# Retention attention and a gated MLP on one core: 64-row chunks on two half-partitions become 128-row chunks on all 128 partitions

## The chip, the cores and the metric

The kernel runs on one core of a Trainium2 chip. The metric is the device time in microseconds (us); the kernel before is given as the median of three runs. Beside the times there is one profiled execution of the kernel, taken by the hardware profiler; its span is a little shorter than the metric.

The engines are named as in the profile: PE (TensorE matmuls), PEld (its weight loads), DVE (VectorE), ACT (ScalarE), POOL (GpSimd) and SP (SyncE, here the engine that issues nearly all DMAs).

## The reference, cut to what matters

```python
# attention: B, H, S, D = 8, 8, 576, 64
scores = q @ k.T / sqrt(D)
gamma  = 1.0 - 2.0 ** (-5.0 - arange(H))
Dmat   = where(rel >= 0, gamma ** rel, 0.0)      # rel = t - s
attn   = (scores * Dmat) @ v                     # no softmax
x      = attn.transpose(0, 2, 1, 3).reshape(B, S, 512)

# gated MLP: w_in [512, 1024], w_sg [576, 576], w_out [512, 512]
h    = gelu(x @ w_in)                            # tanh form
u, v = h[..., :512], h[..., 512:]
v_n  = (v - mean(v)) / sqrt(var(v) + 1e-6) * g_ln
v_s  = einsum('ts,bsd->btd', w_sg, v_n) + b_sg[None, :, None]
out  = x + (u * v_s) @ w_out                     # [8, 576, 512], float32
```

The decay `gamma ** (t - s)` splits into a power of the query's row times a power of the key's row. So attention can go through each sequence chunk by chunk: inside a chunk a masked product of scores and values, and from all earlier chunks one 64x64 state matrix per head.

## The kernel before, in words

All work is cut into jobs, one engine each. An order written out as a long string of job numbers (`ORDER`) says in which sequence the jobs are emitted; `fN` in it puts N units of warming matmuls (`scr`, line 357, on zeros; a unit is 128 columns) on PE. Each engine runs its own instructions in that sequence and waits by semaphores. SP is one such queue: a DMA that waits for its data or for a free buffer holds up the DMAs behind it.

The 8 sequences are done in four pairs. A pair has 1152 rows and is 9 tiles of 128 rows in the MLP (36 tiles in all); the middle tile holds the last 64 rows of the first sequence and the first 64 of the second. In attention a pair is 5 blocks (`RB`): two blocks of 256 rows of the first sequence, the middle block with 64 rows of each, and two blocks of 256 rows of the second. A block's rows lie on 128 partitions as two chunks of 64 rows (in a block of 256 rows a partition holds 2 neighbouring rows), so that all attention matmuls work on 64x64 tiles of PE, four at a time.

What happens to a block, in the names of the profile:

- **Loads** (lines 457 and 460, `ld`, `ldq`): q, k, v of the block from HBM on SP's queue. In a block of 256 rows, two neighbouring rows of 64 floats make one run of 512 B in k and v, and four of q, loaded for two blocks at once (`ldq`), make 1024 B. The middle block's loads have runs of 256 B on 64 partitions each.
- **Prep** (lines 493 and 503): k is cast to bf16 (`kb`), q and v are multiplied by their powers `gpow` (`qb`, `vb`), mostly on POOL.
- **T** (line 540): q and k are transposed by PE into PSUM (`pp`) and copied by DVE (`qT`, `kT`). For the last pair's blocks of 256 rows this is done by four DMA transposes on SP's queue instead (line 560).
- **S** (line 591): scores of the chunk into `pp`; DVE multiplies them by the mask (`ret`, line 604).
- **Z** (line 627): k transposed times v, the chunk's contribution to the state, into `zp`; DVE adds it to the running sum (`run`), and a bf16 copy is made (`zb`).
- **O** (line 673): state times q plus masked scores times v into one `pp`. It comes in two halves, `a_O` and `a_O2`: the second writes the other PSUM bank of each tile, and a semaphore (`swap`) or a drain of PE stands between the two. ACT copies the output, which is x transposed, into `xT` (line 730).

The MLP on a tile:

- `hv` (line 741): x times the v half of `w_in`; gelu on ACT (`vg`), mean and variance on DVE (`bst`, `mv`), four small operations on POOL (`mv`, lines 761 to 764), and the normalised bf16 `vn` (`vmid` for the middle tile) on ACT (line 776).
- `hu` (line 788): the u half of `w_in` times x transposed, gelu on ACT into `uT`.
- `wp` (line 807): `w_sg` along the sequence, times `vn`; per sequence 4 column blocks by 2 halves of 288 rows by 5 tiles, 320 matmuls over all. It needs all tiles of its sequence normalised. DVE multiplies the result into `uT` (line 817). `w_sg` is transposed by PE at the start, once for each sequence of a pair, since their rows lie differently on the tiles (`wtp`, line 921, 50 matmuls).
- `op` (line 838): `uT` times `w_out`. The residual x is added from `xT`: in the first pair by matmuls with the identity (line 833), afterwards from a DMA transpose of `xT` (`xr`, line 847, 27 of them) that DVE adds when it writes `ob` (line 855). `ob` is stored on SP's queue (line 860).

`wp` of the first sequence of a pair can start after the middle block, that of the second after the fifth.

The block's shape, and the load that goes with it, in the code before:

```python
    RB = [(2, 0, ((0, 0), (0, 128))), (2, 2, ((0, 256), (0, 384))),
          (1, MID, ((0, 512), (1, 0))),
          (2, 5, ((1, 64), (1, 192))), (2, 7, ((1, 320), (1, 448)))]
    ...
        if ns == 2:
            e, r0 = ch[0]
            s_ = 4 if sup else 2
            nc.sync.dma_start(f_[:], src[2 * p + e, :, r0:r0 + 128 * s_, :].rearrange("h (p s) d -> p h (s d)", s=s_))
        else:
            for c, (e, r0) in enumerate(ch):
                nc.sync.dma_start(f_[64 * c:64 * c + 64, :, :D], src[2 * p + e, :, r0:r0 + 64, :].rearrange("h p d -> p h d"))
```

Of the kernel before, what the change touches and what calls it, by code (L numbers as in the profile page):

```python
# [19 lines left out]
FETCH = (5400.0, 5000.0)  # L20
# [46 lines left out]
class Job:  # L67
    def __init__(self, eng, dur, due, fn, deps=(), new=None, uses=(), mode=None, nbytes=0, run=0, what="", behind=None, since=0.0, lag=0.0, ins=0, port=False, parts=1):
# [12 lines left out]
class Planner:  # L81
# [50 lines left out]
    def place(self, j, t):  # L132
# [19 lines left out]
        else:  # L152
            late = 0.0
            if j.eng == "PE":
                while self.count + j.ins > 256 * self.block:
# [3 lines left out]
                    self.landed += FETCH[self.landed > 32000.0]  # L159
# [11 lines left out]
    def follow(self, order):  # L171
        line = {e: [] for e in self.free}
        for x in order.split():
            j = self.fill(int(x[1:]), 0.0 if x[0] == "f" and self.warm else 2700.0) if x[0] == "f" else self.jobs[int(x)]
            self.warm = self.warm or x[0] == "f"
            line[j.eng].append(j)
# [58 lines left out]
def kernel(  # L235
# [21 lines left out]
    MID = NT // 2  # L257
    HS = S // 2
    SB = (S + 127) // 128
    NB0 = S - 128 * MID  # L260
# [4 lines left out]
    outf = out.rearrange("b s d -> (b s) d")  # L265

    BUFS = dict(ld=8, ldq=2, qb=2, kb=2, vb=3, qT=2, kT=2, ret=4, zb=6, run=4, xT=2, uT=2, vg=3, mv=3, vn=11, ob=4,
# [6 lines left out]
    def new(tag, shape, dtype):  # L274
# [3 lines left out]
    RB = [(2, 0, ((0, 0), (0, 128))), (2, 2, ((0, 256), (0, 384))),  # L278
          (1, MID, ((0, 512), (1, 0))),
          (2, 5, ((1, 64), (1, 192))), (2, 7, ((1, 320), (1, 448)))]  # L280
    NBK = len(RB)
    XP = 1
    TBQ, TBK = 15, 15
    JOINT = (0, 1)
# [3 lines left out]
    wnat = consts.tile([128, SB, S + 128], BF, name="wnat")  # L288
# [9 lines left out]
    msk4 = consts.tile([128, 2, 4, 32], BF, name="msk4")  # L298
    msk2 = consts.tile([128, 2, 2, 64], BF, name="msk2")
    msk1 = consts.tile([128, 64], BF, name="msk1")  # L300
    NQ, NV = 13, 2 * NBK
    srow_i = consts.tile([128, NQ + NV], I32, name="srow_i")
    srow = consts.tile([128, NQ + NV], F32, name="srow")
    lngt = consts.tile([128, H], F32, name="lngt")
    gpow = consts.tile([128, (NQ + NV) * H], F32, name="gpow")
# [3 lines left out]
    wT = [[consts.tile([128, S], BF, name=f"wT{e}_{j}") for j in range(SB)] for e in range(2)]  # L309
# [7 lines left out]
    nc.gpsimd.iota(srow_i[:, :8], pattern=[[64, 2], [1, 4]], base=-ORG, channel_multiplier=4)  # L317
    nc.gpsimd.iota(srow_i[:, 9:13], pattern=[[256, 2], [1, 2]], base=-ORG, channel_multiplier=2)
    for o, r0 in ((NQ, 0), (NQ + 6, 64)):
        nc.gpsimd.iota(srow_i[:, o:o + 4], pattern=[[-256, 2], [-1, 2]], base=ORG - r0, channel_multiplier=-2)  # L320
    for e in range(2):
        R = slice(64 * e, 64 * e + 64)
        nc.gpsimd.iota(srow_i[R, 8:9], pattern=[[1, 1]], base=RB[2][2][e][1] - ORG, channel_multiplier=1)
        nc.gpsimd.iota(srow_i[R, NQ + 4:NQ + 6], pattern=[[-1, 2]], base=ORG - RB[2][2][e][1], channel_multiplier=-1)
# [5 lines left out]
    def powers(o, n, w):  # L330
        return gpow[:, H * o:H * (o + n * w)].rearrange("p (n h s) -> p n h s", n=n, h=H)

    for o, n, w in ((0, 2, 4), (8, 1, 1), (9, 2 + NBK, 2)):
        g = powers(o, n, w)
        nc.vector.tensor_tensor(g, srow[:, o:o + n * w].rearrange("p (n s) -> p n s", n=n).unsqueeze(2).to_broadcast([128, n, H, w]),
                                lngt[:].unsqueeze(1).unsqueeze(3).to_broadcast([128, n, H, w]), op=Alu.mult)
# [100 lines left out]
    def joint(b):  # L437
        return b % NBK == 2 or b in JOINT

# [766 lines left out]
```

## Time and profile before

| | |
|---|---|
| time, median of 3 runs | 212.62 us (212.53 to 215.94) |
| span of the profiled execution | 211.4 us, 7911 instructions |
| median less span | 1.2 us |
| TensorE's granted clock | full from about 21 us on |
| DMA | 48.4 MB, 85910 packets |

Each line of the profile's groups and of the timeline gives line, engine, operation, output and inputs by name, the tile of PE in rows and columns (64*64, 64*128 or 128*128), and the shape of the output. A group's duration on PE is a latency: matmuls overlap, so the price of one is the distance between the starts of groups. "x16" counts instructions. In rows of windows, the columns are the window, its length, the busy time of PE, PEld, DVE, ACT and POOL with their counts, the granted clock, the mean busy share of the DMA engines (it can exceed 1), and GB/s.

### The profile page before, as it was taken

The numbers are of one execution on the slowest core, as the hardware profiler recorded it, in microseconds if no ns is written. First come the engines' busy times: TensorE is split into PE (matmuls) and PEld (weight loads), VectorE is DVE, ScalarE is ACT, GpSimd is POOL, SyncE is SP. The second block draws the span as 40 slices with busy tenths as digits, with TensorE's granted clock in tenths as the row PEclk, the third lists the DMA queues.
The fourth block names the chain that finished last, engine by engine and source line by source line (L and its number), as shares of the span: only waits on it lengthen the run. The fifth ranks groups of instructions, "written<-read, shape, count | busy, mean of one in ns | idle before, by whom it ended". The sixth has DMA issues, their size and how long they took to land.

```text
span 211.4 us, 7911 instructions
## 1 busy us (share of the span) xinstructions
PE 197.6 (93%) x3384; PEld 137.8 (65%) x3416; DVE 152.5 (72%) x291; ACT 116.8 (55%) x207; POOL 118.3 (56%) x169
## 2 busy tenths in 40 slices
PE   7939999988999999999999999999999999999992
PEld 6727586666676677666767677566677675656661
DVE  3296498877888287967888875897865688576673
ACT  5230598892486954579585452776248349334400
POOL 8735158998667859993769679147582313022000
PEclk9985999999999999999999999999999999999999
DMA  6999999999899999999999999999999902586655
GB/s 164 335 276 305 170 374 295 231 291 340 192 248 296 296 324 276 214 328 189 243 285 109 243 307 206 198 323 182 222 172 148 270 0 78 149 153 174 176 172 198
DMA packets 85910, 48.37 MB, mean 229 GB/s; under 512 B 37035, under 2 KB 79283, under 8 KB 85875
## 3 DMA queue, kind: packets, MB, share of 16 engines
q1 hardware_dynamic: 85856, 47.87, 97.3%
q8 instruction: 26, 0.43, 0.9%
q14 instruction: 10, 0.07, 0.2%
q10 hardware_dynamic: 18, 0.00, 0.0%
HBM read 32.79 MB, written 9.44 MB: 200 GB/s over the span
## 4 chain that ended last, share of the span: by engine, by line
PE 79%; DVE 9%; issue 3%; POOL 3%; DMA 3%; ACT 1%; DVEq 0%; SPq 0%; POOLq 0%
PE wp L807 17%; PE hu L788 13%; PE op L838 13%; PE hv L741 12%; PE scr L357 6%; PE pp L673 6%; PE pp L591 4%; PE pp L540 3%; DMA ld<-in_v_dram 3%; DVE ret L604 2%; PE zp L627 2%; POOL vb L503 1%; DVE bst L756 1%; PE op L833 1%; POOL qb L503 1%
## 5 line engine op out<-in xcount | busy, mean ns | idle before, releaser
L807 PE MATMUL wp<-wT,vn 128*128 128x288 bf16 x256 | 41.1, 286 | 0.7 <-issue 0.6
L503 POOL TENSOR_TENSOR vb<-ld,gpow 128x1024 bf16<-128x1024 f32 (+1 forms) x20 | 34.5, 1731 | 11.6 <-DMA ld<-in_v_dram 8.8
L604 DVE TENSOR_TENSOR ret<-pp,msk 128x1024 bf16<-128x1024 f32 x32 | 38.3, 1215 | 3.4 <-PE pp L591 3.4
L788 PE MATMUL hu<-xT,w_in 128*128 128x256 bf16 (+1 forms) x320 | 36.8, 262 | 0.2
L817 DVE TENSOR_TENSOR uT<-wp,uT 128x288 bf16<-128x288 f32 x64 | 27.6, 451 | 12.4 <-PE wp L807 11.2
L741 PE MATMUL hv<-w_in,xT 128*128 128x512 bf16 x122 | 34.7, 380 | 1.7 <-ACT xT L730 0.3
L838 PE MATMUL op<-w_out,uT 128*128 128x512 bf16 (+1 forms) x138 | 34.4, 373 | 0.6 <-issue 0.2
L776 ACT ACTIVATE vn<-vg,mv 128x512 bf16<-128x512 f32 x32 | 25.3, 809 | 15.3 <-POOL mv L764 15.2
L748 ACT ACTIVATE vg<-hv 128x512 f32<-128x512 f32 x36 | 21.3, 596 | 21.8 <-PE hv L741 16.6
L788 PEld LDWEIGHTS <-w_in 128*128 128x128 bf16 x320 | 28.1, 98 | 7.2 <-issue 0.8
L756 DVE BATCH_NORM_STATS2 bst<-vg 128x6 f32<-128x512 f32 x36 | 24.7, 685 | 9.3 <-ACT vg L748 9.3
L730 ACT ACTIVATE xT<-pp 128x512 bf16<-128x512 f32 (+1 forms) x40 | 20.8, 550 | 18.1 <-PE pp L673 18.1
L807 PEld LDWEIGHTS <-vn 128*128 128x128 bf16 x256 | 24.4, 98 | 9.6 <-issue 0.7
L761 POOL TENSOR_SCALAR mv<-mv 128x2 f32<-128x2 f32 (+1 forms) x20 | 4.5, 224 | 44.7 <-DVE mv L757 37.8
L503 POOL TENSOR_TENSOR qb<-ldq,gpow 128x1024 bf16<-128x1024 f32 x14 | 26.9, 1934 | 4.0 <-DMA ldq<-in_q_dram 4.0
L798 ACT ACTIVATE uT<-hu 128x512 bf16<-128x512 f32 x36 | 21.2, 594 | 13.0 <-PE hu L788 12.9
L855 DVE TENSOR_TENSOR ob<-op,xr 128x512 f32<-128x512 f32 (+1 forms) x28 | 18.4, 669 | 8.3 <-PE op L838 6.3
L838 PEld LDWEIGHTS <-uT 128*128 128x128 bf16 x148 | 13.7, 98 | 11.3
L741 PEld LDWEIGHTS <-xT 128*128 128x128 bf16 x144 | 13.2, 98 | 12.0 <-ACT xT L730 0.2
L807 PE MATMUL wp<-wT,vmid 128*128 128x288 bf16 x64 | 18.0, 287 | 0.1
L357 PE MATMUL scr<-warm 128*128 128x256 f32 (+1 forms) x52 | 16.5, 489 | 1.2 <-DVE warm L316 1.2
L357 PEld LDWEIGHTS scr<-warm 128*128 128x128 f32 x52 | 13.0, 271 | 3.9 <-DVE warm L316 1.2
(100 smaller groups left out, 261.7 us busy)
## 6 DMA issues: line engine op xcount, KB each, us to landing
out_dram<-ob SPq DMA_DIRECT2D x35, 256.0 KB, 3.5
ld<-in_k_dram SPq DMA_DIRECT2D x16, 512.0 KB, 6.9
ld<-in_v_dram SPq DMA_DIRECT2D x16, 512.0 KB, 7.0
ldq<-in_q_dram SPq DMA_DIRECT2D x7, 1024.0 KB, 9.6
xT<-in_moe_w_sg_dram SPq DMA_DIRECT2D x2, 576.0 KB, 8.4
ld<-in_q_dram SPq DMA_DIRECT2D x2, 512.0 KB, 7.0
xT<-in_moe_w_in_dram SPq DMA_DIRECT2D x1, 1024.0 KB, 8.0
ld<-in_k_dram SPq DMA_DIRECT2D x8, 128.0 KB, 6.0
```

Source lines behind the costliest of these rows:

```text
L357: nc.tensor.matmul(scr[:, :w], warm[:, :128], warm[:, :w], start=True, stop=True, skip_group_check=True)
L503: ve.tensor_tensor(dst, src, g.unsqueeze(len(src.shape) - 1).to_broadcast(list(src.shape)), op=Alu.mult)
L604: ins = nc.vector.tensor_tensor(ret[:].rearrange("p r (k t) -> p (r k) t", k=2), sc[:].rearrange("p r (k t) -> p (r k) t", k=2), (msk2 if ...
L741: ins = nc.tensor.matmul(hv[:], xTs[p][:, m, kk, :], w_in[:, kk, F2:], start=(kk == 0), stop=(kk == KK - 1))
L748: unfence(nc.scalar.activation(vgs[i][:], cur.pop(("hv", i))[:], Act.Gelu_apprx_tanh), ("V", i))
L756: nc.vector.bn_stats(bst[:], vgs[i][:])
L776: nc.scalar.activation(vn[:], vg[:], Act.Identity, scale=mv[:, s, 2:3], bias=mv[:, s, 3:4])
L788: ins = nc.tensor.matmul(hu[:, n, :], w_in[:, kk, 128 * c:128 * c + 128], xTs[p][:, m:m + w, kk, :], start=(kk == 0), stop=(kk == KK - 1), ...
L798: unfence(nc.scalar.activation(uTs[p][:, c0:c1, 128 * m:128 * m + 128 * w], cur.pop(("hu", i, half))[:], Act.Gelu_apprx_tanh), ("U", i, half))
L807: ins = nc.tensor.matmul(ps[:], vns[t0 + j][e][:, 128 * c:128 * c + 128], wT[e][j][:, half * HS:(half + 1) * HS], start=(j == 0), stop=(j ...
L817: ins = nc.vector.tensor_tensor(uTs[p][:, c, col:col + HS], cur.pop(("wp", b, c, half))[:], uTs[p][:, c, col:col + HS], op=Alu.mult)
L838: ins = nc.tensor.matmul(op[:], uTs[p][:, c, r], w_out[:, c, cs], start=(p >= XP and c == 0), stop=(c == KK - 1), skip_group_check=True)
```

## The change

**Rows.** A chunk now has 128 consecutive rows, one row on each of 128 partitions. The half block comes first: the first 64 rows of both sequences of the pair, one on each half of the partitions. Four full blocks of two chunks follow (`NS`). In the first pair a full block holds two chunks of one sequence, as before; from the second pair on (`SEQ`) it holds the same chunk of both sequences. The MLP's tiles follow: tile 0 is the half one, then the chunks of both sequences in turn.

**Loads.** A load is one row of 64 floats per partition and head, for q as for k and v, in runs of 256 B.

```diff
-    RB = [(2, 0, ((0, 0), (0, 128))), (2, 2, ((0, 256), (0, 384))),
...
+    NS = [1, 2, 2, 2, 2]
...
+        r0, r1 = rows_of(n)
+        src = dict(q=q, k=k, v=v)[t][2 * p:2 * p + 2]
+        f_ = st[b, t] = new("ld", [128, 2 * H, D], F32)
+        if n and p >= SEQ:
+            nc.sync.dma_start(f_[:], src[:, :, r0:r1, :].rearrange("e h p d -> p (e h) d"))
+        else:
+            for c, (e, kc) in enumerate(parts_of(b)):
+                r0, r1 = rows_of(kc + 1)
+                dst = f_[:, H * c:H * c + H, :] if n else f_[64 * c:64 * c + 64, :H, :]
+                nc.sync.dma_start(dst, src[e, :, r0:r1, :].rearrange("h p d -> p h d"))
```

**Attention on PE.** All transposes are done on PE. Scores of a full block are 16 matmuls on tiles of 64 rows and 128 columns of PE. Z takes 128 rows at once. O is one job: 16 state matmuls on 64x64 tiles, then 16 core matmuls over 128 rows on tiles of 64 columns; `a_O2`, the drain and the `swap` waits are gone.

```diff
+        for n, kk in enumerate((2 * g, 2 * g + 1) if ns == 2 else range(KK)):
+            for r, c in ((0, 0), (1, 0), (0, 1), (1, 1)):
+                if ns == 2:
+                    dst = sc[:, r, (2 * n + c) * 128:(2 * n + c) * 128 + 128]
...
+                nc.tensor.matmul(dst, T_of(b, "k", r, c, kk), T_of(b, "q", r, c, kk), start=True, stop=True, skip_group_check=True)
...
+                    R, s = (slice(0, 128), c) if ns == 2 else (slice(64 * c, 64 * c + 64), 0)
+                    nc.tensor.matmul(z[c][64 * hh:64 * hh + 64, 64 * kk:64 * kk + 64], kb[R, kk, s, hh, :], vb[R, s, KK * hh + kk, :],
...
+        for c in range(2):
+            for k2 in (0, 2):
+                for hh in range(2):
+                    state(k2, hh, c)
+                    state(k2 + 1, hh, c)
+        for c in range(2):
+            for hh in range(2):
+                for kk in range(KK):
+                    core(kk, hh, c)
-    def a_O2(b):
-        on = pend.pop(b)
-        if on is None:
-            nc.tensor.drain()
-        elif on:
-            nc.tensor.wait_ge(swap, on)
```

**MLP.** `w_sg` is transposed once for both sequences (30 matmuls). `wp`'s two halves are 320 and 256 rows. From the second pair on, `wp` of both sequences starts only after the pair's last block. The middle tile's `op` is computed as two times 64 rows, and stored in one DMA of both sequences.

```diff
-    HS = S // 2
+    HALF = ((0, NB0 + 256), (NB0 + 256, S))
...
+            for e in [e] if n else range(2):
+                nc.tensor.matmul(op[:] if n else op[64 * e:64 * e + 64, :], uTs[p][:, c, e, r0:r1], w_out[:, c, cs],
```

**Small operations and engines.** Two of the four POOL operations before the norm remain there, and one (`m_nb`) goes to DVE or POOL. A job may now have alternatives (`alts`), and a number after a colon in `ORDER` picks one: 20 norms and 7 half ones go to POOL, some casts and copies to DVE.

**Buffers and order.** `ld` has 11 buffers (8, and 2 of `ldq`), `qb`, `kb` and `qT` 4 each, `vn` 14 for 11. The order is a new one, with 74 warming units for 47:

```diff
 ORDER = (
-    '1 f3 0 f1 2 f5 f10 3 73 6 f2 75 17 f3 76 103 7 104 72 105 106 77 107 8 78 271 201 4 5 199 f14 272 200 273 16 13 '
...
+    '2 12 1 13 101 79 17 f10 81 8 82 100:1 f3 f3 85 7 83 86 271 84 110 272 273:1 275 80 109 0 6 106 f15 112 3 113 105:1 14 274 f6 f1 99:1 288 205 289 102 '
```

What this does to the order of instructions shows at three places. In the rows, shapes are partitions by elements, and x2 counts instructions.

SP's queue in the middle of the program, where the first stores (`out_dram`) and the second half of the loads stand; before:

```order
L860 DMA out_dram<-ob 128x512
L457 DMA ld<-in_v_dram 128x8x128
L457 DMA ldq<-in_q_dram 128x8x256
L860 DMA out_dram<-ob 128x512
L457 DMA ld<-in_k_dram 128x8x128
L860 DMA out_dram<-ob 128x512
L460 DMA ld<-in_k_dram 64x8x64 x2
```

and with the change:

```order
L476 DMA ld<-in_k_dram 64x8x64 x2
L805 DMA out_dram<-ob 128x512 x2
L471 DMA ld<-in_q_dram 128x16x64
L471 DMA ld<-in_k_dram 128x16x64 x2
L471 DMA ld<-in_v_dram 128x16x64
L476 DMA ld<-in_v_dram 64x8x64 x2
L789 DMA_TRANSPOSE xr<-xT 128x4x128
L805 DMA out_dram<-ob 128x512
```

A load of 8 runs of 128 or 256 floats on a partition has become one of 16 runs of 64, and the transposes of the residual stand among the loads.

SP's queue at the last loads; before:

```order
L457 DMA ld<-in_v_dram 128x8x128
L457 DMA ld<-in_k_dram 128x8x128
L847 DMA_TRANSPOSE xr<-xT 128x4x128 x2
L860 DMA out_dram<-ob 128x512
L847 DMA_TRANSPOSE xr<-xT 128x4x128
L860 DMA out_dram<-ob 128x512
L847 DMA_TRANSPOSE xr<-xT 128x4x128
L560 DMA_TRANSPOSE kT<-kb 128x16x128
L560 DMA_TRANSPOSE qT<-qb 128x16x128
L457 DMA ld<-in_v_dram 128x8x128
L860 DMA out_dram<-ob 128x512
L847 DMA_TRANSPOSE xr<-xT 128x4x128 x2
```

and with the change:

```order
L471 DMA ld<-in_k_dram 128x16x64 x2
L471 DMA ld<-in_q_dram 128x16x64
L789 DMA_TRANSPOSE xr<-xT 128x4x128 x2
L471 DMA ld<-in_v_dram 128x16x64
L789 DMA_TRANSPOSE xr<-xT 128x4x128
L471 DMA ld<-in_k_dram 128x16x64
L805 DMA out_dram<-ob 128x512
L471 DMA ld<-in_v_dram 128x16x64
L805 DMA out_dram<-ob 128x512 x2
L789 DMA_TRANSPOSE xr<-xT 128x4x128 x3
```

The transposes of q and k are gone from the queue. Before the end of the last K load now stand 14 stores and 12 residual transposes in all.

PE about a third of the way through, at a second half of O, which stood apart, here between a Z and the next T; before:

```order
L627 LDWEIGHTS kb_1132
L627 MATMUL zp_1659<-vb_1558,kb_1132 64x64
L673 LDWEIGHTS zb_1556
L673 MATMUL pp_1621<-qT_1387,zb_1556 64x128
L673 LDWEIGHTS zb_1556
L673 MATMUL pp_1621<-qT_1387,zb_1556 64x128
```

and with the change, inside O:

```order
L628 LDWEIGHTS zb_1537
L628 MATMUL pp_1873<-qT_1658,zb_1537 64x128
L628 LDWEIGHTS vb_1687
L628 MATMUL pp_1873<-ret_1827,vb_1687 64x128
L628 LDWEIGHTS vb_1687
L628 MATMUL pp_1873<-ret_1827,vb_1687 64x128
```

State (`zb`) and core (`vb`) matmuls of a block now follow each other directly, on tiles of 64x64 and of 128x64.

More of the change, by code (lines that the diff above doesn't have):

```diff
@@ L67, with __init__ @@
 class Job:
-    def __init__(self, eng, dur, due, fn, deps=(), new=None, uses=(), mode=None, nbytes=0, run=0, what="", behind=None, since=0.0, lag=0.0, ins=0, port=False, parts=1):
+    def __init__(self, eng, dur, due, fn, deps=(), new=None, uses=(), mode=None, nbytes=0, run=0, what="", behind=None, since=0.0, lag=0.0, ins=0, port=False, parts=1, alts=(), grp=None):
+        self.alts, self.grp = list(alts), grp
         self.what, self.behind, self.since, self.lag, self.ins, self.port, self.parts = what, behind, since, lag, ins, port, parts
@@ L417, in sg_load @@
         ld.append(add("SP", 450.0, 0.0, f_last, new=b1, nbytes=64 * S * 4, run=2304))
-        return ld, [add("ACT", 677.0, 0.0, lambda j=j: g(j), deps=[ld[j // 2]], uses=[bA if j < 4 else b1]) for j in range(SB)]
+        return ld, [add("ACT", 677.0, 0.0, al(j)[0][2], deps=[ld[j // 2]], uses=[bA if j < 4 else b1], alts=al(j)) for j in range(SB)]
     def wo_load():
@@ L518, in fence @@
-    def fence(ins, what):
-        if what in fenced:
-            tc.declare_fence(ins.ins, group=fenced[what])
-    def unfence(ins, what, last=True):
-        if what in fenced:
-            tc.declare_no_dep(ins.ins, group=fenced.pop(what) if last else fenced[what],
-                              reason="the last matmul of the same job ends later")
-    def a_T(b, t):
-        tp = psP.tile([128, 2, 1024], BF, name="pp", tag="pp")
-        st[b, "tp", t] = tp
-        ns = RB[b % NBK][0]
-        n = 0
-        parts = [(kb_of(b), 256 * ns), (qb_of(b), 0)] if joint(b) else [(qb_of(b), 0)] if t == "q" else [(kb_of(b), 0), (kb_of(b + 1), 512)]
-        for src, o0 in parts:
-            s_ = src.shape[2]
-            for kk in range(KK):
-                for s in range(s_):
+            dst = st[b, "vb"][:, :ns].rearrange("p s h d -> p (s h) d")
@@ new lines, with a_Z @@
+    runs, zbs = {}, {}
+    def a_Z(b):
+        ns, gs = NS[b % NBK], groups_of(b)
+        z = cur["zp", b] = [psD.tile([128, 256 * ns], F32, name="zp", tag="d") for c in range(3 - ns)]
+        if ns == 2:
+            z = [z[0][:, :256], z[0][:, 256:]]
+        kb, vb = qk_of(b, "k"), st[b, "vb"]
+        begun = set()
+        for kk in range(KK):
+            for c in sum(gs, ()):
+                for hh in range(2):
+                    R, s = (slice(0, 128), c) if ns == 2 else (slice(64 * c, 64 * c + 64), 0)
+                    nc.tensor.matmul(z[c][64 * hh:64 * hh + 64, 64 * kk:64 * kk + 64], kb[R, kk, s, hh, :], vb[R, s, KK * hh + kk, :],
+                                     start=(c % (3 - ns), hh) not in begun, stop=True, skip_group_check=True)
+                    begun.add((c % (3 - ns), hh))
@@ new lines, in a_Zsum, with copy @@
+    def a_Zsum(b, g):
+        p, x = b // NBK, parts_of(b)
+        e, kc = x[g[0]]
+        fin = kc == NBK - 3
+        dst = state_tile(zbs, b, g, "zb", BF) if fin else state_tile(runs, b, g, "run", F32)
+        if kc < 0:
+            nc.vector.tensor_copy(dst, z_of(b, g))
+        else:
+            was, i = runs[p, e, kc - 1]
+            nc.vector.tensor_tensor(dst, z_of(b, g), was[:, 256 * i:256 * (i + len(g))], op=Alu.add)
+    def copy(eng, dst, src):
+        return nc.scalar.activation(dst, src, Act.Copy) if eng == "ACT" else {"DVE": nc.vector, "POOL": nc.gpsimd}[eng].tensor_copy(dst, src)
@@ L665, in a_O, with a_Zev @@
+    def a_Zev(b, g, eng="ACT"):
+        dst = state_tile(zbs, b, g, "zb", BF)
+        if b % NBK == 0:
+            copy(eng, dst, z_of(b, g))
+        else:
+            was, i = runs[(b // NBK, *parts_of(b)[g[0]])]
+            copy(eng, dst, was[:, 256 * i:256 * (i + len(g))])
+    def a_O(b):
+        n = b % NBK
+        ns = NS[n]
         cs = 64 * ns
@@ L1026, with prep @@
-        J["B_k", b] = B_qkb["q", U_] if jn else B_qkb["k", U_]
+        g = "at%d" % b
+        B_vb[b], B_qkT[b] = Buf("vb"), Buf("qT")
+        def prep(b, t, due, buf, ld):
+            fn = lambda e: lambda: a_prep(b, t, e)
+            slow = 1715.0 * h + 190
+            if t == "k":
+                al = [("POOL", 855.0 * h + 183, fn("POOL"), False), ("ACT", 855.0 * h + 190, fn("ACT"), False), ("DVE", 560.0 * h + 120, fn("DVE"), True)]
+            else:
+                al = [("POOL", slow, fn("POOL"), False), ("DVE", 1110.0 * h + 120, fn("DVE"), True)]
+            return add(al[0][0], al[0][1], due, al[0][2], deps=[J["ld", b, t]], new=buf, uses=[B_ld[b, t]], alts=al, grp=g)
@@ L1069 @@
-        own = 580.0 if ns == 2 else 215.0
-        st[b, "zs"] = zs
-        deps = [J["v", b]] + J["tdeps", b] + [J["Se", b, g] for g in range(ns)] + [J[("zb",) + z] for z in zs if z]
-        uses = [B_vb[b], J["B_T", b][0]] + [B_ret[b, g] for g in range(ns)] + [B_zb[z] for z in zs if z]
-        jO1 = add("PE", own, t0 + PR["O"], lambda b=b: a_O(b), deps=deps, new=[otb], uses=uses, mode="Q", what=("O", b), ins=33 * ns + 16)
-        jO = add("PE", 112.0, jO1.due + 300.0, lambda b=b: a_O2(b), deps=[jO1], lag=270.0, uses=uses + [otb], mode="Q", what=("O2", b), ins=18)
+                jzb = add("ACT", 597.0 if two else 395.0, due + 100.0, lambda b=b, g=g: a_Zev(b, g), grp="at%d" % b,
+                          deps=[jz] + ([Z_of[(p, *x[0])][0]] if also else []) if fst else [jr], new=None if also else bz,
+                          alts=[(en, d, lambda b=b, g=g, en=en: a_Zev(b, g, en), en == "DVE" and not fst)
+                                for en, d in (("ACT", 597.0 if two else 395.0), ("DVE", 680.0 if two else 418.0))],
+                          uses=([zpb[g[0]]] if fst else [br]) + ([bz] if also else []))
@@ new lines @@
+            for c in g:
+                Z_of[(p, *x[c])] = (jzb, bz, br, jr)
+        zs = list(dict.fromkeys(Z_of[p, e, kc - 1][:2] for e, kc in x)) if n else []
+        otb = Buf("pp")
+        deps = [J["v", b]] + J["T", b] + [J["Se", b, g] for g in range(ns)] + [z[0] for z in zs]
+        uses = [B_vb[b], B_qkT[b], otb] + [B_ret[b, g] for g in range(ns)] + [z[1] for z in zs]
+        jO = add("PE", 760.0 if ns == 2 else 215.0, t0 + PR["O"], lambda b=b: a_O(b), deps=deps, new=[otb], uses=uses[:2] + uses[3:], mode="Q",
+                 what=("O", b), ins=65 if ns == 2 else 33, grp="at%d" % b)
```

829 lines of the change are left out of this document (361 added, 468 removed), and 57 rows, old and new, of the table ORDER.

## The prediction

> **What bounds the kernel now.** I read the busy times first, then the chain of waits by engine and line, then the windows by stage (columns: length, PE busy, PE loads, DVE, ACT, POOL, granted clock, DMA share, GB/s).
>
> ```profile
> span 211.4 us, 7911 instructions
> PE 197.6 (93%) x3384; PEld 137.8 (65%) x3416; DVE 152.5 (72%) x291; ACT 116.8 (55%) x207; POOL 118.3 (56%) x169
> PE 79%; DVE 9%; issue 3%; POOL 3%; DMA 3%; ACT 1%; DVEq 0%; SPq 0%; POOLq 0%
> 0.00:5.30 5.30, 4.06 (x13) 3.50 (x14) 1.60 (x15) 3.00 (x4) 4.34 (x25) 1.00 0.63 165
> 3.00:94.00 91.00, 83.69 (x1639) 60.19 (x1652) 65.92 (x123) 54.83 (x99) 65.96 (x79) 0.96 1.07 282
> 94.00:166.00 72.00, 70.82 (x1319) 49.16 (x1332) 55.19 (x100) 43.77 (x81) 43.11 (x57) 1.00 1.20 223
> 180.00:200.00 20.00, 19.89 (x148) 12.77 (x139) 12.55 (x27) 8.24 (x14) 2.74 (x8) 1.00 0.70 168
> ```
>
> TensorE is the bound: 93% busy over the span, 98% from 94 to 166 us and 99% from 180 to 200, at the full clock. So a term counts if it changes PE's stream, or if it makes PE wait. The DMA share is above 1 for as long as loads run: they are the second bound, close behind. The chain of waits (start, length, what) shows where PE stood still:
>
> ```profile
> 16.32 5.51 PE scr L357 x14
> 24.19 0.82 PE hv L741 x3
> 36.39 1.09 PE hu L788 x10
> 144.48 5.91 DMA ld<-in_v_dram
> ```
>
> The start, to about 36 us, is paced by data and filled with warming matmuls (`scr`); one late V load holds PE at 144. The profiled execution took 211.4 us and the median of the three runs is 212.62: I make the sum in the span and add 1.2 us.
>
> **PE's matmuls.** Prices come from PE's timeline, as the distance from one group's start to the next one's, since a row's own length includes the pipeline's end.
>
> ```profile
> 86.75 1.03 PE L741 MATMUL hv<-w_in,xT 128*128 128x512 bf16 x4
> 87.71 0.64 PE L540 MATMUL pp<-ident,qb 64*128 64x64 bf16 x32
> 88.28 1.04 PE L741 MATMUL hv<-w_in,xT 128*128 128x512 bf16 x3
> 94.05 1.06 PE L788 MATMUL hu<-xT,w_in 128*128 128x128 bf16 x16
> 95.03 0.42 PE L591 MATMUL pp<-qT,kT 64*64 64x128 bf16 x16
> 95.39 0.64 PE L540 MATMUL pp<-ident,kb 64*128 64x64 bf16 x32
> 101.08 1.92 PE L788 MATMUL hu<-xT,w_in 128*128 128x256 bf16 x16
> 102.83 0.65 PE L807 MATMUL wp<-wT,vn 128*128 128x288 bf16 x4
> 105.63 0.44 PE L627 MATMUL zp<-vb,kb 64*64 64x64 bf16 x32
> 105.90 0.22 PE L673 MATMUL pp<-ret,vb 64*64 64x128 bf16 x1
> 106.35 0.22 PE L591 MATMUL pp<-qT,kT 64*64 64x128 bf16 x1
> 62.02 0.37 PE zp L627 x32
> ```
>
> A column of a full-array matmul costs 0.43 ns: 16 `hu` of 256 columns take 101.08 to 102.83, 1.75 us, and `wp` follows without a gap. So four `hv` take 0.86 us and should end at 87.61, and the transposes begin 0.10 later; 16 `hu` of 128 columns (55.5 ns each, 0.89 us) end at 94.94, and the 64x64 scores begin 0.09 later. These gaps of about 0.1 us come where the tile shape changes, and nowhere between groups of one shape.
>
> - *Scores.* Four 64x64 tiles at work at once make 13.4 ns of each (16 in 0.36 us less a gap). The new tile is 64x128, two at once, so 2 x 13.9 = 27.8 ns. Before 576 x 13.4 = 7.7 us; after 256 x 27.8 + 64 x 13.4 = 8.0. **+0.3.**
> - *Transposes.* 32 take 0.57 us less 0.11: 14.4 ns. PE gets 576 for 448, since the last pair's no longer go through the DMA queue. **+1.8.**
> - *Z.* 480 between 8.4 ns (32 from 105.63 to 105.90) and 11.6 (32 in 0.37), say 10: 4.8 us. After, 256 of all 128 rows, two tiles at once, as the transposes: 14.4 ns, 3.7 us. **-1.1** (-0.3 to -1.9).
> - *Attention output.* 832 x 14 ns (about 32 between 105.90 and 106.35) = 11.6. After 256 state matmuls at 14, 256 core ones over 128 rows at 27.8, and 64 of the half block at 14: 11.6. **0.**
> - *Spatial weights.* One copy for both sequences: 30 transposes for 50, at 55.5 ns. **-1.1.** `wp` splits 576 columns into 256 and 320 instead of 2 x 288: **0**. `hv`, `hu`, `op` keep their columns; the middle tile's `op` comes in two halves of 64 output rows. If those don't run side by side, its four tiles cost up to 3.4 us more; I take 0.
>
> The matmuls alone come to -0.1: a fifth fewer instructions, the same column time.
>
> - *Shape changes.* Along PE's order the shape changes 100 times before and 137 after: state and core matmuls of one block now differ (64x64 against 128x64), and scores, Z and transposes have three shapes. 37 x 0.11 = **+4.1** (0 if the next weights are always loaded under the last matmuls, 5.2 at 0.14).
>
> By the Trainium skill, TensorEngine Tiling (Array Packing), Tiling Modes, a change of tiling mode drains TensorE. The two gaps of about 0.1 us above agree with it.
>
> ```profile
> L673 PE MATMUL pp<-qT,zb 64*64 64x128 bf16 x224 | 9.8, 226 | 1.0 <-DVE ret L604 0.7
> L921 PE MATMUL wtp<-ident,wnat 128*128 128x128 bf16 x50 | 3.8, 220 | 0.2 <-ACT wnat L413 0.2
> POOL mv L761 <- DVE mv L757: 37.8, 9, 10.1
> ```
>
> - *Seams and issue.* The 20 second halves of the attention output, with their semaphore or drain, are gone, and with them the 1.0 us that PE stood before `pp<-qT,zb`: **-1.0**. PE has 18% fewer instructions, and "issue" is 3% of the chain (6.6 us): **-1.2** if it falls alike (0 to -5.4).
> - *Start.* The order gives PE 74 warming units instead of 47, a unit 0.2 us by the 14 double ones in 5.51: +5.3 if they are on the path. Against it, the first block is the half one and its 128 KB arrive sooner (-3). The U half of the first weight stands behind 4.98 MB; at 237 GB/s and with 1.2 MB of other weights it is cast by 32.4, before `hu` starts now (36.39). I take **0**.
> - *Other engines.* DVE gains casts and copies and loses second state copies; I estimate 159 us, 75%. POOL takes 27 norms; it stands 37.8 us before `mv`. Both stay below PE: **0**. If a group of norms came late, `wp` of both sequences, which now start only when the pair's last block is through, would stand first.
>
> Sum: -0.1 + 4.1 - 1.0 - 1.2 = **+1.8**, a span of 213.2 and a time of **214.4 us**.
>
> **The loads.** All of q, k and v, 28.3 MB, now come in runs of 256 B (64 values of one row). Before, 63% came in 512 B, 26% in 1 KB and 11% in 256 B. What each rate was is read from windows in which mostly one kind was under way: 512 B, then weights of 2 KB, then twice 256 B, then 64-row tiles of 256 B:
>
> ```profile
> 5.00:7.00 2.00, 2.00 (x8) 1.62 (x7) 0.00 (x0) 1.36 (x3) 1.77 (x5) 1.00 1.22 290
> 26.00:28.00 2.00, 2.00 (x70) 1.78 (x59) 1.86 (x5) 1.80 (x5) 1.89 (x4) 1.00 1.08 378
> 18.50:19.00 0.50, 0.50 (x3) 0.36 (x2) 0.50 (x2) 0.00 (x0) 0.50 (x1) 0.50 1.22 238
> 21.50:22.00 0.50, 0.50 (x7) 0.23 (x5) 0.00 (x0) 0.00 (x0) 0.00 (x0) 1.00 1.28 235
> 22.00:24.00 2.00, 1.76 (x76) 1.32 (x75) 0.11 (x1) 0.69 (x2) 0.00 (x0) 1.00 1.32 178
> xr<-xT SPq DMA_TRANSPOSE x27, 4.1
> out_dram<-ob SPq DMA_DIRECT2D x2, 128.0 KB, 2.0
> ```
>
> Before: 17.8 MB at 290, 7.3 at 378 (as the weights), 3.2 at 237: 94 us. After: 28.3 at 237 = 119.5, so 25 us more. Is it hidden? In the new order all loads but one V stand ahead of the last K's end, with 14 stores and 12 residual transposes (`xr`) among them. From 94 to 166 us 16.1 MB moved, 4.1 of it transposes'; the other 12.0 at 290 take 41 us, which leaves 31 for 15 `xr` and the four q and k ones (as long as four each): 1.0 us for each. An `xr` that waits on SP for its tile holds the loads behind it too; I count its transfer alone. So the last K has landed at: 2.3 (start: 0.87 MB in 5.3 us, 3.0 of them at 290) + 27.8 MB/237 = 117.3 + weights 4.5 MB/378 = 11.8 + stores 9.7 + `xr` 12 + landing 2.0 = 155. Then come its cast (1.3), and what PE still has after the last transposes. The prices of that are in the rows:
>
> ```profile
> 184.62 0.65 PE L807 MATMUL wp<-wT,vn 128*128 128x288 bf16 x4
> 185.11 0.29 PE L807 MATMUL wp<-wT,vmid 128*128 128x288 bf16 x1
> 185.24 0.65 PE L807 MATMUL wp<-wT,vn 128*128 128x288 bf16 x4
> 185.73 0.29 PE L807 MATMUL wp<-wT,vmid 128*128 128x288 bf16 x1
> 185.85 1.89 PE L838 MATMUL op<-w_out,uT 128*128 128x512 bf16 x8
> 187.57 0.65 PE L807 MATMUL wp<-wT,vn 128*128 128x288 bf16 x4
> ```
>
> 125 `wp` at 0.124 (five in 0.62), 80 `op` at 0.205 (eight in 1.72, some narrower), 24 `hv`, 48 `hu`, and 5 of attention: 46 us. With 5 for gaps and the end, 207.5. That is 5.7 below the sum: the loads are just hidden. Each 10 GB/s less costs about 5.2 us, and below some 226 GB/s they decide.
>
> A rule speaks against the change: the Trainium skill, DMA: Bandwidth & Descriptors, Specifications, gives 512 B as the least transfer for line rate. Its section Why small descriptors are slow (HBM only) puts about 3 cycles on each packet, 11 for 256 B and 19 for 512; 8 and 16 of them data; an estimate by it is 290 x (8/11)/(16/19) = 250 GB/s, 6 us less of loads than I summed. The rows of 235 and 238 are near it, the 178 is not.
>
> **Rivals.**
>
> *1: loads fall behind, slower.* One mechanism: a mean rate below 226 GB/s. For it: 178 GB/s in the third window of 256 B, and 223 from 94 to 166 with transposes inside. Against it: those 178 were 64-row tiles, which reach half the partitions, and the new full blocks fill all. At 215 the loads take 12 us more: 219.5, time **220.7**. PE would stand before transposes in the middle of the run.
>
> *2: fewer seams, faster.* Shape changes hide behind the other tiles' work (-4.1) and the waits at issue go with the second halves (-5.4 in all, 4.2 more than summed). For it: 1,200 fewer instructions on PE (6739 to 5532, loads included). Against it: the gaps above stand beside weight loads that were free to run ahead. 204.9 in the span, time **206.1**.
>
> **How the numbers follow.** About 2% is what a measurement of this kernel can tell from no change: 208.4 to 216.9 us. The forecast (210 to 218.5, by its own terms' bounds) has 0.42, of which 0.14 is slower by over 2%; rival 1 has 0.28, 0.24 of it slower; rival 2 has 0.30, 0.27 of it faster. Together: faster 0.27, same 0.35, slower 0.38. The range goes from rival 2 with a start 2 us earlier, **204**, to loads at 209 GB/s, **224**.
>
> **What would show it.** Right: PE at 93% or more and near 198 us; scores and core matmuls about 28 ns apart; gaps of 0.1 us between state and core matmuls of a block; loads' windows at 230 to 245 GB/s; the last K landed near 155 us, and DMA a small share of the chain. Rival 1 shows as DMA at 8% of the chain or more, with PE idle before transposes; rival 2 as PE busy below 193 us, with state and core matmuls back to back. It would be wrong altogether if `hv` began later than 28 us, or if DVE or POOL took over the chain in the middle of the run.

## The result: 248.06 us, 16% slower

The changed kernel takes 248.06 us (median of four runs, 246.8 to 248.65) against 213.51 for the kernel before on the same chip: a ratio of 1.160, with a 95% interval of 1.152 to 1.168. The forecast of 214.4 and its range up to 224 were both too low.

The profile's page after, by its span, busy times, DMA slices, and the chain of waits by engine and line:

```profile
span 246.9 us, 6687 instructions
PE 210.9 (85%) x2787; PEld 139.1 (56%) x2818; DVE 160.6 (65%) x302; ACT 109.7 (44%) x171; POOL 125.7 (51%) x156
DMA  5999989999989999999996999989999334439942
PE 39%; DMA 22%; SPq 13%; issue 8%; POOL 7%; DVE 4%; ACT 3%; DVEq 0%; ACTq 0%; POOLq 0%
PE wp L758 9%; SPq L476 9%; DMA ld<-in_q_dram 8%; PE hu L737 7%; PE hv L681 7%; DMA ld<-in_v_dram 7%; PE op L783 7%; PE pp L628 3%; POOL qb L505 3%; POOL vb L505 2%; DMA ld<-in_k_dram 2%; DMA out_dram<-ob 2%; DMA xr<-xT 2%; PE pp L549 2%; SPq L807 1%
```

PE is no longer the bound: it fell from 93% of the span to 85%, and from 79% of the chain to 39%. The DMA transfers and SP's queue, 3% of the chain before, are 35% now. The DMA slices are full up to about 190 us; before, they were full to 170. PE is busy for 210.9 us all the same, 13 more than before. Warming matmuls are 5.8 of these (23.5 instead of 17.7). Another part goes with the granted clock, which was below full in windows in which PE stood idle, here from 130 to 140 us and from 160 to 170 (columns as in the prediction: length, PE, PEld, DVE, ACT, POOL, clock, DMA share, GB/s):

```profile
130.00:140.00 10.00, 6.83 (x75) 3.38 (x73) 5.86 (x10) 0.63 (x1) 4.50 (x3) 0.83 0.71 157
160.00:170.00 10.00, 5.26 (x28) 2.23 (x29) 4.59 (x10) 1.96 (x4) 3.12 (x8) 0.66 0.95 201
```

Two windows of the changed kernel in which almost nothing but loads of 256 B runs was under way, two short ones inside the second, and two near the end:

```profile
50.00:60.00 10.00, 9.95 (x121) 6.95 (x121) 7.67 (x16) 5.25 (x8) 7.69 (x10) 1.00 0.97 195
60.00:70.00 10.00, 9.20 (x198) 6.16 (x198) 8.00 (x12) 5.51 (x10) 6.82 (x5) 1.00 0.95 191
64.00:65.00 1.00, 0.41 (x29) 0.31 (x23) 0.87 (x2) 0.84 (x2) 0.35 (x1) 1.00 1.31 241
67.75:68.75 1.00, 1.00 (x10) 0.80 (x9) 1.00 (x3) 0.63 (x3) 1.00 (x1) 1.00 0.17 33
225.00:227.00 2.00, 2.00 (x12) 1.07 (x11) 1.42 (x3) 0.00 (x0) 0.00 (x0) 1.00 0.21 51
242.00:245.00 3.00, 0.00 (x0) 0.00 (x0) 0.00 (x0) 0.00 (x0) 0.00 (x0) 0.50 0.15 51
```

The loads ran at a mean of 191 to 195 GB/s, not at the 237 that the forecast used. The mean share of 0.95 to 0.97 doesn't say that the engines were never idle: it is made of stretches such as the one at 241 GB/s and of pauses such as the one at 33. What sets the pauses no run took apart. And near the end there are stretches in which the DMA moved 51 GB/s with four fifths of its engines idle, while work waited for it. The last K's cast (POOL's timeline) and its transposes (PE's) came late:

```profile
183.48 1.04 POOL L503 CAST kb<-ld 128x1024 bf16<-128x1024 f32 x1 [5.71 <-DMA ld<-in_k_dram]
184.57 0.41 PE L518 MATMUL pp<-ident,kb 64*128 64x64 bf16 x16 [1.84 <-POOL kb L503]
```

The forecast had the last K landed at 155 us, here it was 183.5. From those transposes to the end it had 51 us (46 and 5), here it was 62.3. SP's timeline and two pieces of the chain show what held the end:

```profile
219.79 0.61 SPq L807 DMA_DIRECT2D out_dram<-ob  x1
220.45 1.22 SPq L789 DMA_TRANSPOSE xr<-xT  x1
223.07 0.82 SPq L805 DMA_DIRECT2D out_dram<-ob  x2
223.93 6.57 SPq L789 DMA_TRANSPOSE xr<-xT  x3
236.55 0.56 SPq L807 DMA_DIRECT2D out_dram<-ob  x1
237.24 2.19 SPq L805 DMA_DIRECT2D out_dram<-ob  x3
```

```profile
223.07 5.62 DMA out_dram<-ob
228.79 3.57 DMA xr<-xT
```

Both slow stretches follow line 807, the store of a half tile of both sequences as one DMA of 2x64x512. 51 GB/s is what two engines move: the trace's packets of 2 KB last 84 ns, 24 GB/s on one engine, and from 225 to 227 us there were 50 of them, two at a time.

### The profile page after: what moved, and what is told of

The parts are those of the page before. It is cut to its first block, busy times and chain, and to the rows that moved or that the text cites. A ratio compares the mean times of both kernels' runs of the same rounds, so it can differ in the third digit from the quotient of the medians.

```text
span 246.9 us, 6687 instructions
## 1 busy us (share of the span) xinstructions
PE 210.9 (85%) x2787; PEld 139.1 (56%) x2818; DVE 160.6 (65%) x302; ACT 109.7 (44%) x171; POOL 125.7 (51%) x156
## 4 chain that ended last, share of the span: by engine, by line
PE 39%; DMA 22%; SPq 13%; issue 8%; POOL 7%; DVE 4%; ACT 3%; DVEq 0%; ACTq 0%; POOLq 0%
PE wp L758 9%; SPq L476 9%; DMA ld<-in_q_dram 8%; PE hu L737 7%; PE hv L681 7%; DMA ld<-in_v_dram 7%; PE op L783 7%; PE pp L628 3%; POOL qb L505 3%; POOL vb L505 2%; DMA ld<-in_k_dram 2%; DMA out_dram<-ob 2%; DMA xr<-xT 2%; PE pp L549 2%; SPq L807 1%
## 5 line engine op out<-in xcount | busy, mean ns | idle before, releaser
L758 PE MATMUL wp<-wT,vn 128*128 128x256 bf16 (+1 forms) x256 | 42.2, 295 | 0.0
L783 PE MATMUL op<-w_out,uT 128*128 128x512 bf16 (+2 forms) x151 | 37.8, 416 | 0.6
L764 DVE TENSOR_TENSOR uT<-wp,uT 128x320 bf16<-128x320 f32 (+1 forms) x64 | 27.0, 449 | 13.3 <-PE wp L758 12.9
L505 POOL TENSOR_TENSOR qb<-ld,gpow 128x1024 bf16<-128x1024 f32 (+1 forms) x17 | 30.2, 1775 | 10.6 <-DMA ld<-in_q_dram 10.3
L607 ACT ACTIVATE xT<-pp 128x512 bf16<-128x512 f32 (+1 forms) x28 | 15.0, 570 | 24.4 <-DVE xT L607 9.3
L797 DVE TENSOR_TENSOR ob<-op,xr 128x512 f32<-128x512 f32 (+1 forms) x28 | 18.4, 667 | 10.7 <-PE op L783 5.7
L783 PEld LDWEIGHTS <-uT 128*128 128x128 bf16 (+1 forms) x164 | 14.6, 108 | 15.9 <-issue 5.0
L528 ACT ACTIVATE qT<-pp 128x2048 bf16<-128x2048 bf16 (+1 forms) x11 | 18.0, 1644 | 11.0 <-PE pp L518 11.0
L371 PE MATMUL scr<-warm 128*128 128x128 f32 (+2 forms) x66 | 21.2, 455 | 1.2 <-DVE warm L336 1.2
L758 PE MATMUL wp<-wTm,vmid 128*128 128x320 bf16 (+1 forms) x64 | 18.8, 294 | 3.0 <-DVE ob L797 2.9
L503 POOL CAST kb<-ld 128x1024 bf16<-128x1024 f32 (+1 forms) x11 | 11.3, 1023 | 12.4 <-DMA ld<-in_k_dram 12.4
```

What stands on the lines that cost most here:

```text
L371: nc.tensor.matmul(dst, warm[:, :128], src, start=True, stop=True, skip_group_check=True)
L505: ve.tensor_tensor(dst, src, g.to_broadcast(list(src.shape)), op=Alu.mult)
L758: nc.tensor.matmul(ps[:], vns[i][e][:, 128 * c:128 * c + 128], wT[:, j - 1, lo:hi] if j else wTm[e][:, lo:hi], start=(j == 0), stop=(j == ...
L764: nc.vector.tensor_tensor(u, cur.pop(("wp", b, c, half))[:], u, op=Alu.mult)
L783: nc.tensor.matmul(op[:] if n else op[64 * e:64 * e + 64, :], uTs[p][:, c, e, r0:r1], w_out[:, c, cs], start=(i >= XT and c == 0), stop=(c ...
L797: nc.vector.tensor_tensor(ob[:, cs], op[:], cur["xr", i][:].rearrange("p j r -> p (j r)")[:, cs], op=Alu.add)
```

## The experiments

The theories, as they stood after the result. **A**: runs of 256 B bound the DMA to some 200 GB/s, and the loads decide. **D**: the 2x64x512 store runs on 2 of 16 engines, holds what is queued behind it and lands last. The rivals: **B**, the new order's stores and transposes ahead of the loads on SP decide, at any rate; **C**, PE's shape changes and seams cost more than summed.

The runs come from several chips. The kernel before took 213.5 us beside the changed kernel, 215.5 beside the first four runs below, 213.9 beside the next four and 212.5 beside the last, so a difference between times of two such groups is uncertain by 2 to 3 us. Where one is used below, the ratios to the kernel before are given too.

### Run length alone, in the changed kernel

```diff
-            nc.sync.dma_start(f_[:], src[:, :, r0:r1, :].rearrange("e h p d -> p (e h) d"))
+            x0 = NB0 + 256 * ((n - 1) // 2)
+            nc.sync.dma_start(f_[:].rearrange("p (h s) d -> p h (s d)", s=2),
+                              src[(n - 1) % 2, :, x0:x0 + 256, :].rearrange("h (p s) d -> p h (s d)", s=2))
```

The loads of the first pair and of the half blocks were cut likewise.

> The changed kernel with every load of q, k and v in runs of 512 B instead of 256 B: same bytes, same tiles, same queue and order. A partition gets other rows than its own, so the values are not the reference's. Theory A (the loads decide, and a run of 256 B holds a DMA engine for 20 ns, which bounds 16 engines to some 200 GB/s): at the 290 GB/s of 512 B the 28.3 MB take 98 us instead of 145, the last K lands near 140 instead of 183, and PE's own sum decides: 216 to 224 us. Rival B (the new order puts stores and residual transposes ahead of loads on SP's queue, and what stands in front there decides, whatever the rate): 238 us or more. Rival C (PE's shape changes and seams cost more than summed): no less than 240.

Measured: 227.6 us, 1.057 times before (1.048 to 1.066). That is 20.5 us less by the length of the runs alone (22 by the ratios 1.160 and 1.057), which no version of B or C gives; but not the 216 to 224 that A alone had expected. Its windows and the last K's cast:

```profile
50.00:60.00 10.00, 9.89 (x124) 6.91 (x124) 8.62 (x18) 4.59 (x8) 8.16 (x10) 1.00 1.11 256
60.00:70.00 10.00, 9.19 (x196) 6.34 (x197) 8.01 (x14) 6.22 (x13) 5.08 (x5) 1.00 0.98 289
```

```profile
165.04 1.04 POOL L507 CAST kb<-ld 128x1024 bf16<-128x1024 f32 x1 [3.39 <-DMA ld<-in_k_dram]
```

The loads run at a mean of 256 to 289 GB/s, and the last K comes 18.4 us sooner. From there to the end of the span it is still 60.6 us, and the store stands there.

The same with 4 KB, `flat[2048 * n - 2048:2048 * n].rearrange("(p s) d -> p (s d)", s=2 * H)`:

> The changed kernel with the loads in runs of 4 KB per partition (2 KB in the first pair's and the half blocks' loads): same bytes and tiles, other rows, so the values are not the reference's. Theory A: loads at about 380 GB/s are out of the way; the time is PE's sum plus the end: 214 to 222 us, within 3 us of the 512 B version. If it is 6 us or more below that one, loads still decided there. Rival B: 238 or more. Rival C: 240 or more.

Measured: 224.92 us, 2.7 less than with 512 B. Runs longer than 512 B bring little, as A expects; again it stays above 222.

### Run length alone, in the kernel before

```diff
-            nc.sync.dma_start(f_[:], src[2 * p + e, :, r0:r0 + 128 * s_, :].rearrange("h (p s) d -> p h (s d)", s=s_))
+            x0 = 0 if sup else 2048 * half_of(b)
+            nc.sync.dma_start(f_[:].rearrange("p h (s d) -> p (h s) d", s=s_),
+                              src[2 * p + e].rearrange("h p d -> (h p) d")[x0:x0 + 1024 * s_].rearrange("(x p) d -> p x d", p=128))
```

> The kernel before with its k, v and q loads of 512 B and 1 KB runs cut into runs of 256 B: same bytes, tiles, queue and order; other rows, so the values are not the reference's. Theory A: 25.2 MB at 195 GB/s take 129 us instead of 81, so the last V lands 35 to 45 us later than its 150 and 240 to 255 us come out. Rival B (order) and rival C (PE's shapes): the old order and the old shapes are all there, so 212 to 222 us.

Measured: 243.67 us against 215.51 for the kernel before beside it, 1.132 times (1.121 to 1.142). Nothing of the old order, shapes or stores had changed. Its page:

```profile
span 242.8 us, 7918 instructions
PE 49%; DMA 18%; POOL 10%; SPq 7%; issue 7%; ACT 5%; DVE 2%; DVEq 0%; POOLq 0%
```

The chain of the kernel before turns into that of the changed one: PE from 79% to 49%, DMA from 3% to 18%. This is the plainest evidence for A: only the run length differs. Whether a run of 256 B is slow on an engine or leaves more pauses in the queue, it doesn't say.

### The half tile's store in two

```diff
-            nc.sync.dma_start(out[2 * p:2 * p + 2, r0:r1, cs], cur["ob", i][:, cs])
+            for e in range(2):
+                nc.sync.dma_start(out[2 * p + e, r0:r1, cs], cur["ob", i][64 * e:64 * e + 64, cs])
```

> The changed kernel with the store of the middle tile (both sequences' 64 rows in one DMA, 2x64x512) written as two DMAs of 64x512. Theory D: the one DMA runs on 2 of 16 engines (49 GB/s in the trace's last microseconds, 5.3 us for 256 KB), holds the residual transposes behind it at 220 to 232 us and is the last to land at the end; in two it takes under 2 us: 4 to 9 us less, 239 to 244. If the 49 GB/s come from 64 rows of 2 KB as such, two DMAs are no better: 246 to 249.

Measured: 232.44 us (230.56 to 233.54), 15.6 us less than the changed kernel (18 by the ratios 1.160 and 1.076). The mechanism was as expected and its price almost twice the upper end. The issues by kind, and the last K's cast and transposes:

```profile
out_dram<-ob SPq DMA_DIRECT2D x10, 128.0 KB, 2.3
```

```profile
176.67 1.04 POOL L503 CAST kb<-ld 128x1024 bf16<-128x1024 f32 x1 [5.01 <-DMA ld<-in_k_dram]
177.76 0.41 PE L518 MATMUL pp<-ident,kb 64*128 64x64 bf16 x16 [1.95 <-POOL kb L503]
```

A half now lands in 2.3 us. The last K comes 6.8 us sooner (two of the four stores stand ahead of it), and from its transposes to the end it is 54.0 us instead of 62.3 (the other two stand there). My expectation had counted the end alone. A likely reading of the stores ahead of the last K: at 18 ns for a packet of 256 B, loads at 195 GB/s keep about 14 of the 16 engines at work, so the two that have 64 packets of 84 ns more, 5.4 us, hold up each load. Four such stores would then make up to 21.5 us, and 15.6 were measured; which engine held up which load the trace doesn't show.

The Trainium skill, DMA: Bandwidth & Descriptors, Why a DMA increments its semaphore by 16 and not by 1, says how many engines a DMA gets: the largest number up to 16 that divides the size of the slowest dimension over 1 on both sides. For a store of 2x64x512 that is 2. The 51 GB/s and this run agree with it.

### Both, and what is left for PE

> The changed kernel with both: loads in 512 B runs (other rows, so the values are not the reference's) and the middle tile's store in two DMAs. If loads and store are two separate costs that add up, and PE's sum of 213 us of span holds: the 227.6 of the 512 B version less some 8 to 12 for the stores, as its end (60 us after the last K) still holds two of them: 215 to 220 us. If the store's price only showed because the 256 B loads kept the DMA queue full: no lower than 224.

Measured: 217.07 us (216.88 to 217.26). The costs add up, though each takes part of the other with it: the store is worth 10.5 us when loads run at 512 B, 15.6 at 256 B and 7.0 at 4 KB (8, 18 and 5 by the ratios).

> The changed kernel with loads in runs of 4 KB (2 KB in the first pair and the half blocks; other rows, so the values are not the reference's) and the store in two DMAs: both DMA costs are out of the way and what is left is PE. By the forecast's own sum (span 213.2, less some start, since the first loads come in sooner): 208 to 216 us. If shape changes and seams cost more than summed: 218 or more; if they were hidden: 206 or less.

Measured: 217.9 us (216.64 to 218.08), 1.022 times before (1.014 to 1.030): just above the upper end, and the same as with 512 B. So this is about what PE makes of the change, with both DMA costs out of the way. Its page, and PE's timeline in one block:

```profile
span 216.1 us, 6725 instructions
PE 204.6 (95%) x2818; PEld 136.4 (63%) x2818; DVE 161.9 (75%) x302; ACT 109.8 (51%) x171; POOL 125.2 (58%) x156
PE 74%; POOL 9%; DVE 5%; DMA 5%; SPq 3%; issue 2%; ACT 1%; POOLq 0%; DVEq 0%; ACTq 0%
```

```profile
27.00 1.03 PE L681 MATMUL hv<-w_in,xT 128*128 128x512 bf16 x4
29.07 0.42 PE L628 MATMUL pp<-qT,zb 64*64 64x128 bf16 x16
29.41 0.64 PE L628 MATMUL pp<-ret,vb 128*64 128x128 bf16 x16
29.98 0.40 PE L549 MATMUL pp<-qT 64*128 64x128 bf16 x8
30.31 0.92 PE L371 MATMUL scr<-warm 128*128 128x256 f32 x4
```

State (16 at 14 ns, 0.22) takes 0.34 with the gap behind it, core (16 at 27.8, 0.44) takes 0.57, and eight scores (0.22) 0.33: prices and gaps of 0.11 to 0.13 as forecast. The span is 2.9 above the sum of 213.2.

### Shape changes

```diff
         for c in range(2):
             for k2 in (0, 2):
-                for hh in range(2):
-                    state(k2, hh, c)
-                    state(k2 + 1, hh, c)
-        for c in range(2):
-            for hh in range(2):
-                for kk in range(KK):
-                    core(kk, hh, c)
+                for f in (state, core):
+                    for hh in range(2):
+                        f(k2, hh, c)
+                        f(k2 + 1, hh, c)
```

> As the 4 KB version with two stores (values not the reference's), but state and core matmuls of a block alternate in four groups of 8 instead of one of 16 each: 96 more changes of PE's tile shape over the 16 full blocks, the same matmuls. At 0.12 us a change: 11 us more than the version without, 10 to 13. If a change of shape is hidden behind the other tiles' work: 0 to 3 more.

Measured: 228.77 us (227.75 to 229.82), 10.9 more than the version without, or 0.113 us for each of the 96 changes. Both versions ran on the same chip. PE's timeline shows them:

```profile
29.29 0.25 PE L628 MATMUL pp<-qT,zb 64*64 64x128 bf16 x4
29.47 0.30 PE L628 MATMUL pp<-ret,vb 128*64 128x128 bf16 x4
29.70 0.25 PE L628 MATMUL pp<-qT,zb 64*64 64x128 bf16 x4
29.88 0.30 PE L628 MATMUL pp<-ret,vb 128*64 128x128 bf16 x4
```

Four state matmuls (0.06 us of work) take 0.18, four core ones (0.11) take 0.23. Nothing of a change is hidden, so the forecast's price was right, C falls, and rival 2's condition with it.

### Transposes on the queue

```diff
-        nc.sync.dma_start_transpose(cur["xr", i][:], xTs[p][:, m].rearrange("p j r -> p (j r)"))
+        nc.sync.dma_start(cur["xr", i][:], xTs[p][:, m])
```

> The changed kernel with two stores and the 27 residual transposes on the DMA queue replaced by plain copies of the same 128 KB (the residual is then not transposed, so the values are not the reference's). If a transpose holds the queue for 1.0 us, as the forecast had it, and stretches the packets beside it, a copy (0.4 us at 300 GB/s) gives back 0.6 us for the 12 ahead of the last K and 3 us or more at the end: 220 to 227 against 232.4. If the transposes cost no more than their bytes: 229 to 234.

Measured: 222.59 us (221.47 to 223.29), 9.8 less than with transposes (7 by the ratios 1.076 and 1.045). The last K's transposes on PE:

```profile
169.55 0.41 PE L518 MATMUL pp<-ident,kb 64*128 64x64 bf16 x16 [0.25 <-POOL kb L503]
```

They start 8.2 us sooner, with 12 `xr` ahead of the last K: 0.7 us more for a transpose than for a copy of the same bytes. With the copy's estimated 0.4, the forecast's 1.0 was about right. This part of B holds: what stands ahead of the loads counts, once the loads decide.

### Warming units

The last 26 units were taken out of the order string of the 4 KB version.

> The version with loads of 4 KB runs and two stores (values not the reference's), without the last 26 of the order's 74 warming units, those that stand on PE from about 22 us on. The forecast took the start at 0 with +5.3 us as its upper end, if the 27 more units lie on the path; the version with them took 217.9, 2.3 more than forecast plus what its own sum leaves. If the units lie on the path, 2 to 5 us go: 213 to 216. If PE waits for data there anyway: 217 to 218.5. If PE's clock falls without them: more than 219.

Measured: 218.66 us, 1.025 times before (1.020 to 1.031), against 1.022 with them. No gain, but no clean test either. PE's clock in the same window, with the units and without them:

```profile
27.00:36.00 9.00, 9.00 (x156) 6.54 (x155) 7.64 (x13) 6.68 (x11) 2.76 (x5) 1.00 0.73 259
27.00:36.00 9.00, 8.42 (x76) 3.54 (x76) 6.81 (x11) 4.90 (x8) 2.59 (x4) 0.52 0.77 283
```

Without them the first `hv` came at 27.16 us (27.00 with them), after PE had waited 1.74 for a copy of `xT` on DVE: the units didn't hold it up. But then PE ran at half the clock to about 36 us, and its first `hu` came at 37.37 instead of 34.78. Over the whole span, too, the mean clock of its executions was 0.964 to 0.984, with the units 0.997 to 1.0. The expectation's third case, a falling clock, is what the trace shows, though the time stayed just under the 219 named for it. What the units cost and what they save can't be told apart here.

## Why the prediction was wrong, step by step

- **The bound.** PE bounds the kernel before, and "the second bound, close behind" were the loads. Both right; what "close" was worth was not.
- **The rate of 256 B runs: the term that failed.** The forecast took 237 GB/s as a mean from two windows of 0.5 us (238 and 235, at shares of 1.22 and 1.28). Such a window shows a dense stretch and not the mean: the changed kernel's loads, too, moved 241 in one microsecond and 33 in another, but 195 and 191 over 10 us. The forecast had a lower number in its own fence, 178 over 2 us, and set it aside because those tiles had 64 rows; loads that were mostly of 128 rows reached only 195. The prediction's estimate of 250 by packet cycles lay further off still, and the measurement decides. With 195, its own line reads 2.3 + 27.8 MB/195 (142.6) + 11.8 + 9.7 + 12 + 2.0 = 180.4 instead of 155, and the run with two stores measured the last K's cast at 176.7. The span becomes 207.5 + 25.3 = 232.8, and that run's was 231.8. The method of the chain was right, and one number in it was a fifth too high.
- **The half tile's store: a term that was missing.** It stood in the list of changes as "stored in one DMA of both sequences", but the sum had no line for it. It cost 15.6 us. The row that could have priced it did not exist in the trace before, where every store had 128 rows as its outermost dimension. The Trainium skill's rule on a DMA's engines, told above with its section, speaks against just this edit; of the DMA rules, the forecast had drawn on those on run length alone.
- **PE's sum.** Right in its prices. Scores, state and core took what was forecast, and shape changes 0.113 us against 0.11. The middle tile's `op` in two halves was put at 0, and eight of its matmuls took 0.89 us from their start to the next group's (84.19 to 85.08 in the run with 4 KB and two stores). Four full ones are 0.86 at the prediction's price, so the halves ran side by side. Of Z, 192 matmuls and not 256 have 128 rows, worth 0.3 us. The time with both DMA costs gone is 217.9, 3.5 above the forecast of 214.4 and within the 210 to 218.5 of its own terms.
- **The start, put at 0: too low.** In the changed kernel the first `hv` came at 29.59 us instead of 24.19, past the 28 that the forecast had named as a sign against itself. With loads of 4 KB and two stores it came at 27.00, so about half of the delay went with them. The 2.8 us left would be most of the 3.5, but that they are the cause wasn't tested.
- **Transposes on the queue, 1.0 us each.** About right: 0.7 more than a copy, by the start of the last K's transposes.
- **DVE and POOL.** DVE was put at 159 us and took 160.6. Neither became the bound.
- **Rival 1** came about in its mechanism, "a mean rate below 226 GB/s", with the sign that was named for it (DMA at 8% of the chain or more; it was 22%). It was priced at 220.7 because its rate was taken at 215, not at the slowest row. At 178 the chain gives 27.8/178 = 156, 39 us more: 246 of span. That this meets the measured 246.9 is chance, since the store's cost isn't in it. The bound from the slowest row was known and was left out of the range.
- **Rival 2** was wrong: nothing of a shape change is hidden. What the vanished seams gave back, summed at 2.2 us, no run measured by itself.

The 33.7 us between forecast and result are then: 15.6 for the store, 14.5 for 256 B runs (232.44 to 217.9, or 12 by the ratios; 20.5 if taken away first), and 3.5 of PE and start, each uncertain by the 2 to 3 us between chips. No version of the changed kernel beat the one before. Even with both DMA costs gone it takes 1.014 to 1.030 times as long. By the sum, that is because the instructions saved on PE save no columns, while 37 more shape changes at 0.113 us cost 4.

## What to carry to other kernels

Read a transfer rate from a window long enough to hold whole transfers (10 us here), and where two rows for one kind disagree, let the slower one bound the range. A layout that puts one row on each partition pays for it in the length of the DMA's runs; when the queue is nearly full, price that before counting instructions on PE. For every DMA that a change touches, stores too, look at its outermost dimension: a 2 there kept the store on 2 of 16 engines, and the kernel was 15.6 us slower for four such stores.

## What the runs showed of the hardware

- A packet's median length in the traces' DMA records was 18 ns for 256 B, 28 to 29 for 512 B, 46 for 1 KB, 84 for 2 KB and 159 for 4 KB: about 9 ns and 0.037 ns for a byte. One after another at 18 ns, packets of 256 B on 16 engines would move 228 GB/s. That is neither a bound nor a mean: records overlap (shares up to 1.3), single microseconds showed 241 and 33, and 10 us of loads 191 to 195.
- One DMA on two engines among loads on sixteen cost 3.9 us each time (15.6 for four) at 256 B runs, 2.6 at 512 B and 1.8 at 4 KB (4.5, 2.0 and 1.2 by the ratios). Its 256 KB spread evenly would be 0.7 us at 378 GB/s.
- A change of PE's tile shape between 64x64 and 128x64 cost 0.113 us, in a stream of matmuls that the timeline shows without waits.
- PE's granted clock was 0.83 and 0.66 in windows in which it had stood idle for data, and 0.52 against 1.00 from 27 to 36 us without the warming units.
